# A list scheduler inside the kernel sets the order of every engine and the buffer of every tile

## The chip, the cores and the metric

The kernel runs on one core of a Trainium2 chip. The metric is the device time of one execution in microseconds (us). Before the change the median of three runs is 337.51 us (337.26 to 338.6).

The engines of the core are named as the profile names them: PE (TensorE, the matrix multiplier; PEld is its loading of weights), ACT (ScalarE), DVE (VectorE), POOL (GpSimd) and SP (SyncE, which issues the transfers of inputs and outputs). Each takes its instructions strictly in the order in which the program lists them; an instruction that has to wait holds up everything behind it on the same engine.

## The reference, cut to what matters

```
f = sigmoid(f_logit)                                   # q, k, v, f_logit: (4, 8, 768, 48)
for t in range(768):
    state = f[t][:, None] * state + outer(k[t], v[t])  # state: (4, 8, 48, 48)
    y[t]  = q[t] @ state
x = y as rows of 384 (8 heads x 48)                    # (3072, 384)
p = domain_probs / sum(domain_probs)                   # 4 experts
out = sum over e of p[:, e] * (relu(x @ w1[e]) @ w2[e])   # w1: 384 x 1024, w2: 1024 x 384
```

A gated linear attention is followed by four small two-layer networks (experts), all four of which are computed for every row and added up with weights p.

## The kernel before

Time is cut into C = 6 chunks c of T = 128 steps; each has B = 4 batches b. For one chunk and one batch the attention is a chain across the engines:

- `gate` (ACT, Exp and Ln; for two batches at once in all chunks but the first) makes log-gates `gp`.
- `pe_cs` (PE) sums them up over time; `exps` (ACT: `eQ`, `eK`, `egs`) makes the factors.
- `products` multiplies q and k by them (`qp`, `kp`; the q product on DVE in chunk 0 and on POOL later, the k product always on POOL); `cast_v` makes `vb`.
- `pe_tp` (PE) transposes both, `ev_tp` (DVE) copies them out of PSUM (`QK`).
- `pe_at` (PE) makes the 128 x 128 products of all heads (`A`), `ev_at` (DVE) masks them (`AT`), one instruction for eight heads.
- `pe_y` (PE) makes the output from `AT`, `vb` and the state of the chunk before, `ev_y` (ACT) copies it (`yb`); `pe_xt` transposes it and `ev_xt` (ACT) copies it into `xT`, the input of the experts.
- `pe_kv` (PE), `ev_kv` (DVE) and `state` (POOL, four instructions) carry the state into the next chunk.

The experts of a chunk are "units" of PE work: 8 h units per expert (`mm_h`, three matmuls of 128x512, result `hp`; the relu goes to DVE for three of eight and to ACT for the others) and 8 o units per expert (`mm_o`, four matmuls of 128x384, result `op`; every second one is followed by its scaling into `o_sb`, on ACT for the first expert and on DVE for the others). An h unit for half of the batches has 128x256 matmuls.

The order is written out by hand. `first_attention` places the steps of chunk 0 at times that are sorted. From then on `units(c)` lists the units of chunk c, alternating h of one expert with o of the expert before, and the attention of chunk c+1 hangs on the units as `steps`: after unit i come the steps that were put at i. Chunk 1 is different: its batches 0 and 1 (LO) go at the end of chunk 0 (steps 29 to 39), its batches 2 and 3 (HI) go into the first units of chunk 1 itself, whose experts 0 and 1 are done for LO first and for HI after (L355 to L359, L443 to L448), and chunk 2 follows from unit 18 of chunk 1 (L437).

Transfers: SP issues all inputs (`load`), first those of chunk 0 one batch at a time, then f, k, q, v of chunks 1 and 2, two batches at a time; later chunks are issued when chunk c starts. The f load of chunk 1 waits for the sixth weight transfer, and with it, being first, everything behind it on SP (L414, L415). The eight weight transfers (`weights`, w1 and w2 of four experts, cast to bf16 on the way) are issued by POOL, after the last k product of chunk 0; the first of them waits for the last k load of chunk 0.

PSUM has eight banks: two for `hp`, two for `op`, two for the small attention results (`pt`) and two for `A`.

## Time and profile before

| what | value |
|---|---|
| median of three runs | 337.51 us (337.26 to 338.6) |
| the profiled execution: its own time | 336.81 us |
| the profiled execution: span from first to last instruction | 335.1 us |
| granted TensorE clock, mean over the span | 0.995 |
| PE busy | 309.5 us (92%), 2304 matmuls |
| DVE / ACT / POOL busy | 159.5 / 148.7 / 95.8 us |
| bytes moved | 30.31 MB |

In the rows quoted below, a timeline row has the start in us from the beginning of the span, the duration in us, engine, source line, operation, output and inputs, the shape, the number of equal instructions merged (x), and in brackets how long the engine had been idle before and what ended that. Matmuls overlap in the records, so the time from the start of one row to the start of the next is the price of it. A row of the windows has the stretch, its length, and for each engine the busy time and the number of instructions in it; then the granted TensorE clock, the DMA share and GB/s. A row of the groups has the number of instructions and after the bar their busy time in us, the mean of one in ns, and the idle time before them.

### The profile page before, as it was taken

What the parts mean: (1) busy time and instruction counts of PE and PEld (TensorE: products, weight loads), DVE (VectorE), ACT (ScalarE), POOL (GpSimd) and SP (SyncE); (2) the same over time, 40 slices, a digit from 0 to 9 for tenths busy, and PEclk for the clock granted to TensorE, in tenths of its full rate; (3) what the DMA queues carried; (4) which work ended last, traced back from release to release, by engine and by line L of the source; (5) the groups of instructions that cost most, each with busy time, mean ns of one, the idle gap of its engine ahead of it and who ended that gap; (6) DMA issues with size and microseconds to landing.
All of it is one profiled execution on the core that took longest, in us unless ns stands there. A gap on an engine that the chain in (4) does not pass through costs nothing.

```text
span 335.1 us, 5754 instructions
## 1 busy us (share of the span) xinstructions
PE 309.5 (92%) x2304; PEld 181.2 (54%) x2304; DVE 159.5 (48%) x259; ACT 148.7 (44%) x299; POOL 95.8 (29%) x164
## 2 busy tenths in 40 slices
PE   2859999976859999999999999999999999999995
PEld 2634555544637665555655555655555555555552
DVE  5664233463533665444565354566454454422442
ACT  5633432607474533645433735533735434244220
POOL 5293400235445532243432143422142200000000
PEclk9999999999998999999999999999999999999999
DMA  8989999999892089022098020000020000110002
GB/s 163 213 116 207 208 202 207 221 206 253 157 210 49 2 163 167 23 72 49 3 186 144 23 72 0 2 2 1 23 73 0 3 0 2 47 49 0 0 2 94
DMA packets 111531, 30.31 MB, mean 90 GB/s; under 512 B 102800, under 2 KB 109968, under 8 KB 111504
## 3 DMA queue, kind: packets, MB, share of 16 engines
q1 hardware_dynamic: 105744, 23.65, 35.6%
q0 software_dynamic: 5760, 6.29, 11.2%
q8 instruction: 18, 0.29, 0.4%
q14 instruction: 9, 0.07, 0.1%
HBM read 31.51 MB, written 4.72 MB: 108 GB/s over the span
## 4 chain that ended last, share of the span: by engine, by line
PE 86%; ACT 4%; DMA 3%; DVE 3%; POOL 3%; issue 1%; POOLq 0%; DVEq 0%; ACTq 0%
PE hp L304 38%; PE op L320 36%; PE pt L194 3%; DMA w_sb<-in_moe_w_dram 2%; PE A L212 2%; POOL kp L177 2%; PE pt L247 1%; PE pt L233 1%; PE pt L229 1%; PE pt L150 1%; PE pt L273 1%; ACT eQ L161 1%; DVE Sf L257 1%; ACT ex L141 1%; DMA fg<-in_f_logit_dram 1%
## 5 line engine op out<-in xcount | busy, mean ns | idle before, releaser
L304 PE MATMUL hp<-xT,w_sb 128*128 128x512 bf16 (+1 forms) x624 | 159.5, 368 | 4.4 <-ACT xT L279 1.1
L320 PE MATMUL op<-w_sb,h_sb 128*128 128x384 bf16 x768 | 154.9, 326 | 0.0
L312 ACT ACTIVATE h_sb<-hp 128x512 bf16<-128x512 f32 (+1 forms) x130 | 73.5, 566 | 98.6 <-PE hp L304 92.5
L320 PEld LDWEIGHTS <-h_sb 128*128 128x128 bf16 x768 | 74.7, 98 | 65.9
L304 PEld LDWEIGHTS <-w_sb 128*128 128x128 bf16 x624 | 57.0, 100 | 45.3 <-issue 7.2
L310 DVE TENSOR_SCALAR h_sb<-hp 128x512 bf16<-128x512 f32 (+1 forms) x78 | 50.6, 649 | 54.8 <-PE hp L304 48.4
L330 DVE SCALAR_TENSOR_TENSOR o_sb<-op,pn,o_sb 128x384 f32<-128x384 f32 x72 | 44.4, 617 | 67.7 <-PE op L320 60.3
L175 POOL TENSOR_TENSOR qp<-qg,eQ 128x384 bf16<-128x384 f32 x20 | 19.9, 997 | 105.2 <-ACT eQ L161 76.8
L265 POOL TENSOR_TENSOR Sf<-Sf,egs 48x192 f32<-48x192 f32 x40 | 20.1, 503 | 52.2 <-DVE Sf L257 50.0
L218 DVE TENSOR_TENSOR AT<-A,mask 128x1024 bf16<-128x1024 f32 x24 | 29.3, 1222 | 8.2 <-PE A L212 7.9
L201 DVE COPY QK<-pt 112x1024 bf16<-112x1024 bf16 x24 | 16.6, 690 | 21.8 <-PE pt L194 21.8
L177 POOL TENSOR_TENSOR kp<-kg,eK 128x384 bf16<-128x384 f32 x24 | 24.1, 1004 | 9.8 <-ACT egs L168 9.8
L239 ACT CAST yb<-pt 128x384 bf16<-128x384 f32 x24 | 11.6, 483 | 25.2 <-PE pt L233 25.2
L257 DVE TENSOR_TENSOR Sf<-Sf,pt 48x192 f32<-48x192 f32 x40 | 14.1, 352 | 15.4 <-PE pt L247 14.6
L279 ACT COPY xT<-pt 128x384 bf16<-128x384 bf16 x20 | 9.5, 477 | 22.5 <-PE pt L273 22.5
L327 ACT ACTIVATE o_sb<-op,pn 128x384 f32<-128x384 f32 x24 | 14.0, 584 | 9.2 <-PE op L320 8.6
L161 ACT ACTIVATE eQ<-pt 128x384 f32<-128x384 f32 x20 | 9.8, 490 | 15.4 <-PE pt L153 11.6
L266 POOL CAST sb<-Sf 48x192 bf16<-48x192 f32 x40 | 13.6, 340 | 2.6
L233 PE MATMUL pt<-vb,AT 128*128 128x48 bf16 x192 | 12.0, 190 | 1.7 <-DVE vb L185 1.7
L194 PE MATMUL pt<-ident,qp 128*112 128x128 bf16 x96 | 10.8, 241 | 2.4 <-DVE qp L175 2.0
L194 PEld LDWEIGHTS <-qp 128*112 128x112 bf16 x96 | 9.4, 146 | 5.8 <-DVE qp L175 2.9
L194 PE MATMUL pt<-ident,kp 128*112 128x128 bf16 x96 | 10.8, 241 | 1.8 <-POOL kp L177 1.8
(52 smaller groups left out, 177.6 us busy)
## 6 DMA issues: line engine op xcount, KB each, us to landing
w_sb<-in_moe_w_dram POOLq DMA_DIRECT2D x8, 768.0 KB, 17.1
out_dram<-o_sb SPq DMA_DIRECT2D x24, 192.0 KB, 1.9
fg<-in_f_logit_dram SPq DMA_DIRECT2D x10, 384.0 KB, 5.8
kg<-in_k_dram SPq DMA_DIRECT2D x10, 384.0 KB, 5.8
qg<-in_q_dram SPq DMA_DIRECT2D x10, 384.0 KB, 5.8
vg<-in_v_dram SPq DMA_DIRECT2D x10, 384.0 KB, 5.6
fg<-in_f_logit_dram SPq DMA_DIRECT2D x4, 192.0 KB, 3.7
kg<-in_k_dram SPq DMA_DIRECT2D x4, 192.0 KB, 3.8
```

Source lines behind the costliest of these rows:

```text
L175: lead.tensor_tensor(out=Qpad[c % NB][:, b, :, 0:D], in0=t["q"][:, bs, :], in1=eQ.rearrange("t (h d) -> t h d", d=D), op=ALU.mult)
L177: nc.gpsimd.tensor_tensor(out=Kpad[c % NB][:, b, :, 0:D], in0=t["k"][:, bs, :], in1=eK.rearrange("t (h d) -> t h d", d=D), op=ALU.mult)
L194: nc.tensor.transpose(out=tp[:, j, i, :], in_=src[:, b, 2 * i:2 * i + 2, :].rearrange("t h d -> t (h d)")[:, 0:MP], identity=ident)
L201: nc.vector.tensor_copy(out=QK, in_=t["tp", b])
L218: nc.vector.tensor_tensor(out=AT.rearrange("s r i t -> s (r i t)"), in0=t["A", b].rearrange("s r i t -> s (r i t)"), in1=mask01, op=ALU.mult)
L257: nc.vector.tensor_tensor(out=Sf[ps, b], in0=Sf[ps, b], in1=KV[ps, :, r, :], op=ALU.add)
L265: nc.gpsimd.tensor_tensor(out=Sf[ps, b], in0=Sf[ps, b], in1=eg, op=ALU.mult)
L304: nc.tensor.matmul(out=hp[:, n0:n1], lhsT=w1_sb[:, e, kk, fc * 128:(fc + 1) * 128], rhs=t["xT"][:, kk, n0:n1], start=(kk == 0), stop=(kk = ...
L310: nc.vector.tensor_relu(out=hs[:, fc, n0:n1], in_=hp[:, n0:n1])
L312: nc.scalar.activation(out=hs[:, fc, n0:n1], in_=hp[:, n0:n1], func=AF.Relu)
L320: nc.tensor.matmul(out=op, lhsT=t["h", e][:, fc, nt * T:(nt + 1) * T], rhs=w2_sb[:, e, fc, :], start=(fc == 0), stop=(fc == KF - 1))
L330: nc.vector.scalar_tensor_tensor(out=o, in0=op, scalar=pe, in1=o, op0=ALU.mult, op1=ALU.add)
```

## The change

Each step of the kernel becomes an `Op` of a `Plan`: with the engines that may run it and its estimated duration on each, a priority, the steps it depends on, the buffers it takes and the buffers it frees. `Plan.run` steps through an estimated time: whenever an engine is free, it takes the step of lowest priority number whose dependencies have ended, plus a latency of 0.2 us to another engine and another 0.2 us behind PE steps, and for which buffers are free. What comes out is the order in which everything is issued, the engine for the steps that may run on several, and the buffer of each tile. "DMA" is one more engine of the plan, which moves one transfer at a time.

Beside the order, these things change:

- `A` is split by r into two banks and its mask into two DVE instructions of 128x512; the attention has a pool of four single banks (`ps_t`) for everything.
- The q and k products and the v cast of chunks 0 and 1 may run on POOL or DVE; the copies `yb` and `xT`, the relu and the scaling of the first expert may run on ACT or DVE. ACT is asked first, so most relus go to ACT.
- `qp`, `kp`, `vb` have 6, 7 and 7 one-batch buffers, `gp` and the inputs four two-batch buffers. Twenty memsets on DVE at the beginning instead of nine.
- The steps of `pe_kv` of chunk 0 stand in its attention, not between its first h units.
- Chunk 1 is planned as four batches in a row, as early as its inputs are estimated to be there, and not as two by two.
- Only the first f load of chunk 1 still depends on the sixth weight transfer.

The core of the diff:

```diff
--- before.py
+++ after.py
...
+    LATENCY = 0.2
...
+    def ready(self, o, e):
+        t = 0.0
+        for d in o.deps:
+            if d.end is None:
+                return None
+            t = max(t, d.end + d.lag + (self.LATENCY if d.engine != e else 0.05))
+        return t
...
+    def take(self, o):
+        new = [k for k in o.takes if k not in self.slot]
+        for r in {k[0] for k in new}:
+            if len(self.rooms[r]) < sum(k[0] == r for k in new):
+                return False
+        for k in new:
+            self.slot[k] = self.rooms[k[0]].pop(0)
+        return True
...
+        left = sorted(self.ops, key=lambda o: o.prio)
+        free_at = {e: 0.0 for o in left for e in o.costs}
+        freeing, done, now = [], [], 0.0
+        while left:
+            for f in [f for f in freeing if f[0] <= now + 1e-9]:
+                freeing.remove(f)
+                self.rooms[f[1]].append(f[2])
+            for e in free_at:
+                while free_at[e] <= now + 1e-9:
+                    for o in left:
+                        if e in o.costs:
+                            t = self.ready(o, e)
+                            if t is not None and t <= now + 1e-9 and self.take(o):
+                                break
+                    else:
+                        break
+                    left.remove(o)
+                    o.engine, o.start, o.end = e, now, now + o.costs[e]
+                    free_at[e] = o.end
+                    for k in o.frees:
+                        self.left[k] -= 1
+                        if self.left[k] == 0:
+                            freeing.append((o.end + self.LATENCY, k[0], self.slot[k]))
+                    done.append(o)
...
-    io = ctx.enter_context(tc.tile_pool(name="io", bufs=2))
...
+    rooms = {"ps_h": 2, "ps_o": 2, "ps_t": 4, "f": 4, "q": 4, "k": 4, "v": 4, "ex": 2, "gp": 4, "e": 2, "qp": 6, "kp": 7,
+             "vb": 7, "egs": 8, "QK": 2, "AT": 2, "yb": 2, "xT": 2, "h": 2, "o": 8}
+    P = Plan(rooms)
...
-    mask01 = const.tile([T, H * T], FP32)
+    mask01 = const.tile([T, NP * T], FP32)
...
+        ins[c, nm, b] = nc.sync.dma_start(out=tl(nm, c, b // 2)[:, hh(b, n), :],
+                                          in_=srcs[nm][c, :, b * H:(b + n) * H, :])
+        if (c, nm, b) == (1, "f", 0):
+            after(ins[c, nm, b], ins["w", 5])
...
+        nc.vector.tensor_tensor(out=tl("AT", c, b)[:, r].rearrange("s i t -> s (i t)"),
+                                in0=tl("A", c, b, r).rearrange("s i t -> s (i t)"), in1=mask01, op=ALU.mult)
...
+    def add_load(c, nm, b, n, prio, deps=()):
+        op = P.add(f"ld {nm}{c}.{b}", {"DMA": 1.05 * n}, lambda e: load(c, nm, b, n), prio,
+                   deps=deps, takes=[(nm, c, b // 2)], lag=2.0)
+        for i in range(n):
+            ld[c, nm, b + i] = op
+        return op
...
+    for i, (e, which) in enumerate(nw):
+        iss = P.add(f"w issue {i}", {"POOL": 0.9}, lambda _, i=i, e=e, which=which: load_w(i, e, which),
+                    -500 + i, deps=[ld[0, "k", B - 1]])
+        wd[e, which] = wd[i] = P.add(f"w {i}", {"DMA": 4.8}, lambda _: None, -500 + i, deps=[iss], lag=2.0)
+    for half in range(2):
+        for j, nm in enumerate("fkqv"):
+            add_load(1, nm, 2 * half, 2, -400 + 4 * half + j, deps=[wd[5]] if half == 0 and j == 0 else [])
...
+            cs = P.add(f"cs {c}.{b}", {"PE": 0.36 if more else 0.17}, on(pe_cs), s(0),
+                       deps=[G[b]], takes=[pt_("cs")], lag=0.2, frees=[("gp", c, half)])
+            ex = P.add(f"exps {c}.{b}", {"ACT": 1.1}, on(exps), s(0) + 0.1, deps=[cs],
+                       takes=[("e", c, b)] + ([("egs", c, b)] if more else []), frees=[pt_("cs")])
+            pe = {"POOL": 1.0, "DVE": 0.56} if c < 2 else {"POOL": 1.0}
+            qm = P.add(f"q {c}.{b}", pe, one(product, 0), s(4) - 0.2,
+                       deps=[ex, ld[c, "q", b]], takes=[("qp", c, b)], frees=[("q", c, half), ("e", c, b)])
+            km = P.add(f"k {c}.{b}", pe, one(product, 1), s(4) - 0.1,
+                       deps=[ex, ld[c, "k", b]], takes=[("kp", c, b)], frees=[("k", c, half), ("e", c, b)])
+            vb = P.add(f"v {c}.{b}", {"POOL": 0.5, "DVE": 0.36} if c < 2 else {"POOL": 0.5}, one(cast_v), s(4),
+                       deps=[ld[c, "v", b]], takes=[("vb", c, b)], frees=[("v", c, half)])
...
+            eA = [P.add(f"ev_at{r} {c}.{b}", {"DVE": 0.7}, on(ev_at, r), s(7) + 0.1 + 0.1 * r, deps=[at],
+                        takes=[("AT", c, b)], frees=[pt_("A", r)]) for r in range(2)]
+            y = P.add(f"y {c}.{b}", {"PE": 0.4 if c else 0.28}, on(pe_y), s(11), deps=eA + [vb, kvdone.get((c - 1, b))],
+                      takes=[pt_("y")], frees=[("QK", c, b), ("AT", c, b), ("vb", c, b)], lag=0.2)
+            ey = P.add(f"ev_y {c}.{b}", {"ACT": 0.48, "DVE": 0.56},
+                       lambda e, b=b: copy(e, tl("yb", c, b), tl("y", c, b)[:, 0:HD]), s(11) + 0.1,
+                       deps=[y], takes=[("yb", c, b)], frees=[pt_("y")])
...
+                kvdone[c, b] = P.add(f"state {c}.{b}", {"POOL": 1.75}, on(state), s(15) + 0.2,
+                                     deps=[ek, ex], frees=[("egs", c, b)])
...
+        m = P.add(f"h {c}.{e}.{fc}.{n0}", {"PE": 0.645 * n / NT}, lambda _: mm_h(c, e, fc, n0, n1), p,
+                  deps=[wd[e, 1]] + [xdone[c, b] for b in xs], takes=[key], lag=0.2, frees=[("xT", c)])
+        hdone[c, e, fc, n0] = P.add(f"relu {c}.{e}.{fc}.{n0}",
+                                    {"ACT": 0.6, "DVE": 0.69} if n == NT else {"ACT": 0.39, "DVE": 0.42},
+                                    lambda g: relu(c, e, fc, n0, n1, g), p - 3, deps=[m],
+                                    takes=[("h", c, e)], frees=[key])
...
-    def weights():
-        for w in ((0, 1), (1, 1), (0, 2), (2, 1), (1, 2), (3, 1), (2, 2), (3, 2)):
-            w_ins.append(load_w(*w))
-        after(w_ins[0], k_last)
...
+    attention(0, lambda b, s: -200 + 3.6 * b + s * 0.8, 1)
...
+            base = u0 + (0 if c else 10)
+            attention(c + 1, lambda b, s, base=base: base + 2 + 5 * b + s, 2)
...
+    done = P.run()
...
+    for o in done:
+        o.emit(o.engine)
...
```

What this does to the lists is shown at three places, before and after.

POOL, from its first product to the second weight issue (`w1_sb`, `w2_sb` are the weights, `Sf` and `egs` belong to `state`). Before:

```order
L177 TENSOR_TENSOR kp0_131<-kg_92,eK_161 128x8x48
L177 TENSOR_TENSOR kp0_131<-kg_92,eK_189 128x8x48
L177 TENSOR_TENSOR kp0_131<-kg_92,eK_240 128x8x48
L177 TENSOR_TENSOR kp0_131<-kg_92,eK_297 128x8x48
L124 DMA w1_sb_148<-in_moe_w1_dram 128x3x1024 x2
```

After:

```order
L257 TENSOR_TENSOR qp0_92<-q0_136,e0_151 128x8x48
L257 TENSOR_TENSOR qp1_94<-q0_136,e1_183 128x8x48
L261 CAST vb0_224<-v0_162 128x384
L257 TENSOR_TENSOR kp2_108<-k1_196,e0_208 128x8x48
L257 TENSOR_TENSOR qp2_96<-q1_215,e0_208 128x8x48
L308 TENSOR_TENSOR Sf_121<-Sf_121,egs0_154 48x192
L309 CAST sb1_125<-Sf_121 48x4x48
L308 TENSOR_TENSOR Sf_121<-Sf_121,egs0_154 48x192
L309 CAST sb1_125<-Sf_121 48x4x48
L225 DMA w1_sb_130<-in_moe_w1_dram 128x3x1024 x2
```

POOL's part of the fourth batch went to DVE, and the state of batch 0 stands ahead of the weights.

SP, behind the load of the probabilities (`pt` in both), where chunk 1 begins. Before:

```order
L83 DMA pt_110<-in_moe_domain_probs_dram 128x24x4
L70 DMA fg_390<-in_f_logit_dram 128x16x48
L70 DMA kg_392<-in_k_dram 128x16x48
L70 DMA qg_394<-in_q_dram 128x16x48
L70 DMA vg_396<-in_v_dram 128x16x48
```

After:

```order
L359 DMA pt_127<-in_moe_domain_probs_dram 128x24x4
L218 DMA k2_338<-in_k_dram 128x16x48
L218 DMA f2_675<-in_f_logit_dram 128x16x48
L218 DMA q2_696<-in_q_dram 128x16x48
L218 DMA v2_714<-in_v_dram 128x16x48
```

The k load now stands ahead of the f load, which is the one that waits for the weights.

ACT, from the second factors of chunk 1's LO batches on (`eQ_776` before, `e1_763` after) to the Ln of the next gate or two. Before:

```order
L161 ACTIVATE eQ_776<-pt_770 128x384
L163 ACTIVATE eK_778<-pt_770 128x384
L168 ACTIVATE egs_759<-pt_770 112x4
L239 CAST yb_875<-pt_857 128x384
L239 CAST yb_906<-pt_888 128x384
L279 COPY xT_924<-pt_920 128x3x128
L279 COPY xT_924<-pt_926 128x3x128
L312 ACTIVATE h_sb_947<-hp_943 128x256
L312 ACTIVATE h_sb_947<-hp_954 128x256
L141 ACTIVATE ex_959<-fg_390 128x768
L143 ACTIVATE gp1_133<-ex_959 128x16x48
```

After:

```order
L251 ACTIVATE e1_763<-ps_t3_743 128x384
L252 ACTIVATE e1_763<-ps_t3_743 128x384
L254 ACTIVATE egs5_766<-ps_t3_743 112x4
L236 ACTIVATE ex1_804<-f3_735 128x768
L240 ACTIVATE gp3_90<-ex1_804 128x16x48
L251 ACTIVATE e0_857<-ps_t2_839 128x384
L252 ACTIVATE e0_857<-ps_t2_839 128x384
L254 ACTIVATE egs6_860<-ps_t2_839 112x4
L251 ACTIVATE e1_878<-ps_t1_845 128x384
L252 ACTIVATE e1_878<-ps_t1_845 128x384
L254 ACTIVATE egs7_881<-ps_t1_845 112x4
L212 COPY xT1_927<-ps_t1_908 128x3x128
```

The gate of the HI batches (`ex`, `gp`) moved from behind the LO batches' `xT` and two relus to ahead of them, and `yb` went to DVE.

More of the change, by code (lines that the diff above doesn't have):

```diff
@@ L61 @@
-    cur = {}
-    def load(c, names, b0, b1):
-        t = cur.setdefault(c, {})
-        ins = []
-        for nm in names:
-            if nm not in t:
-                t[nm] = io.tile([T, B * H, D], FP32, name=nm + "g")
-            hs = slice(b0 * H, b1 * H)
-            ins.append(nc.sync.dma_start(out=t[nm][:, hs, :], in_=srcs[nm][c, :, hs, :]))
-        return ins
-    def after(later, earlier):
-        tc.add_manual_dep(later.ins, earlier.ins.name,
-                          mybir.DependencyInfo(mybir.DependencyClass.Sync, mybir.DependencyReason.DATA),
-                          reason="order of transfers")
@@ new lines, in after, with flat, hh, copy @@
+    def after(later, earlier):
+        tc.add_manual_dep(later.ins, earlier.ins.name,
+                          mybir.DependencyInfo(mybir.DependencyClass.Sync, mybir.DependencyReason.DATA),
+                          reason="order of transfers")
+    def flat(t, i):
+        return t[:, 2 * i:2 * i + 2, :].rearrange("t h d -> t (h d)")
+    def hh(b, n=1):
+        return slice((b % 2) * H, (b % 2 + n) * H)
+    def copy(eng, out, in_):
+        if eng == "ACT":
+            nc.scalar.copy(out=out, in_=in_)
+        else:
+            engines[eng].tensor_copy(out=out, in_=in_)
```

522 lines of the change are left out of this document (232 added, 290 removed).

## The prediction

> **What bounds the kernel now.** I read the page first, then the busy time by stages, then the timeline of the stages that are not full.
>
> ```profile
> span 335.1 us, 5754 instructions
> PE 309.5 (92%) x2304; PEld 181.2 (54%) x2304; DVE 159.5 (48%) x259; ACT 148.7 (44%) x299; POOL 95.8 (29%) x164
> PE   2859999976859999999999999999999999999995
> ```
>
> PE bounds it: 92% busy, the others below half. The slices show where it isn't full: the first three (to 25 us), slices 8 to 12 (59 to 101 us), and the last. By stages:
>
> ```profile
> 25.00:33.40 8.40, 8.25 (x39) 3.81 (x40) 3.89 (x9) 2.99 (x5) 2.80 (x8) 1.00 1.21 207
> 33.40:64.20 30.80, 30.80 (x172) 16.39 (x170) 11.43 (x19) 12.72 (x21) 3.96 (x10) 1.00 1.22 209
> 64.20:104.00 39.80, 29.87 (x302) 21.08 (x300) 17.58 (x31) 19.42 (x47) 18.66 (x31) 0.96 1.08 200
> 100.00:102.00 2.00, 1.48 (x10) 1.12 (x9) 0.42 (x1) 0.98 (x4) 1.99 (x3) 0.54 0.63 122
> 102.00:104.00 2.00, 2.00 (x19) 1.67 (x17) 1.12 (x2) 0.38 (x1) 0.41 (x1) 0.60 0.50 102
> 119.20:325.20 206.00, 206.00 (x1484) 116.56 (x1483) 99.92 (x154) 91.76 (x175) 46.83 (x80) 1.00 0.21 45
> ```
>
> From 119.2 to 325.2 PE has no idle time: nothing is to be had there, only lost. The hole is 64.2 to 104, the passage from chunk 0 to chunk 1: 39.80 - 29.87 = **9.93 us idle**, and 4 us at a granted clock of 0.54 and 0.60. No engine is full there. What PE waits for:
>
> ```profile
> 69.70 0.43 PE L194 MATMUL pt<-ident,kp 128*112 128x128 bf16 x4 [0.52 <-POOL kp L177]
> 72.62 0.40 PE L212 MATMUL A<-QK 48*128 48x128 bf16 x8 [0.75 <-DVE AT L218]
> 79.48 0.83 ACT L141 ACTIVATE ex<-fg 128x768 f32<-128x768 f32 x1
> 81.24 0.32 PE L150 MATMUL pt<-gp,Ub 128*128 128x384 bf16 x1 [1.63 <-ACT gp L143]
> 95.91 0.84 ACT L141 ACTIVATE ex<-fg 128x768 f32<-128x768 f32 x1
> 97.67 0.32 PE L150 MATMUL pt<-gp,Ub 128*128 128x384 bf16 x1 [1.12 <-ACT gp L143]
> 99.55 0.49 PE L304 MATMUL hp<-xT,w_sb 128*128 128x256 bf16 x3 [1.05 <-ACT h_sb L312]
> 56.36 1.58 SPq L70 DMA_DIRECT2D fg<-in_f_logit_dram  x1
> 63.38 1.82 SPq L70 DMA_DIRECT2D fg<-in_f_logit_dram  x1
> fg<-in_f_logit_dram SPq DMA_DIRECT2D x10, 384.0 KB, 5.8
> ```
>
> Links of the attention chain follow each other with too little PE work between. Yet the HI gate starts at 79.48 although its f load was issued at 56.36 and, by the median of 5.8, landed at 62; chunk 2's (issued 63.38, landed about 69) starts at 95.91. The hand-written order, not a transfer, holds them.
>
> **The start.** This changes most in order, and costs.
>
> ```profile
> 14.75 0.68 SPq L83 DMA_DIRECT2D pt<-in_moe_domain_probs_dram  x1
> 18.23 1.71 POOL L124 DMA_DIRECT2D w_sb<-in_moe_w_dram  x2
> 24.39 0.48 ACT L279 COPY xT<-op 128x384 bf16<-128x384 bf16 x1 [0.59 <-PE op L273]
> 25.10 4.43 PE L304 MATMUL hp<-xT,w_sb 128*128 128x512 bf16 x12 [0.75 <-DMA w_sb<-in_moe_w_dram]
> 29.56 1.46 PE L304 MATMUL hp<-xT,w_sb 128*128 128x512 bf16 x6
> 31.27 1.46 PE L304 MATMUL hp<-xT,w_sb 128*128 128x512 bf16 x6
> 6.42 1.00 POOL L177 TENSOR_TENSOR kp<-kg,eK 128x384 bf16<-128x384 f32 x1 [2.09 <-ACT egs L168]
> L201 DVE COPY QK<-pt 112x1024 bf16<-112x1024 bf16 x24 | 16.6, 690 | 21.8 <-PE pt L194 21.8
> L310 DVE TENSOR_SCALAR h_sb<-hp 128x512 bf16<-128x512 f32 x66 | 45.5, 690 | 39.2 <-PE hp L304 34.1 <-ACT ex L141 4.2
> L175 DVE TENSOR_TENSOR qp<-qg,eQ 128x384 bf16<-128x384 f32 x4 | 2.2, 558 | 3.2 <-ACT eQ L161 2.6 <-DMA qg<-in_q_dram 0.6
> L257 DVE TENSOR_TENSOR Sf<-Sf,pt 48x192 f32<-48x192 f32 x40 | 14.1, 352 | 15.4 <-PE pt L247 14.6
> L185 DVE CAST vb<-vg 128x384 bf16<-128x384 f32 x4 | 1.5, 376 | 0.0
> L218 DVE TENSOR_TENSOR AT<-A,mask 128x1024 bf16<-128x1024 f32 x24 | 29.3, 1222 | 8.2 <-PE A L212 7.9
> L265 POOL TENSOR_TENSOR Sf<-Sf,egs 48x192 f32<-48x192 f32 x40 | 20.1, 503 | 52.2 <-DVE Sf L257 50.0 <-ACT o_sb L327 0.3
> L312 ACT ACTIVATE h_sb<-hp 128x512 bf16<-128x512 f32 x110 | 65.8, 598 | 89.0 <-PE hp L304 82.9 <-DVE o_sb L330 5.2 <-ACT xT L279 0.4
> L330 DVE SCALAR_TENSOR_TENSOR o_sb<-op,pn,o_sb 128x384 f32<-128x384 f32 x72 | 44.4, 617 | 67.7 <-PE op L320 60.3
> ```
>
> The first h unit needs both the first weights (issued 18.23, waited for until 25.10) and the last `xT` (24.39 + 0.48). Half a mask instruction appears in no row: at least 1.22 / 2 = 0.61, and for the same shape read from PSUM the relu's 0.69. I take 0.69, so a pair costs 0.16 more, 3.8 us over 24, all beside other work except in the two stages computed here.
>
> DVE's new list from its first product to the fourth mask holds four products (2.23), four QK copies (2.76), eight half masks (5.52), three casts (1.13), six state additions (2.11): 13.75 us. Ready at 6.4 (the factors, as POOL's first product at 6.42 shows), it ends at 20.2 if DVE never waits. Followed hop by hop, with each producer's row, it ends at 23.5: the q transposes of batches 0 to 2 now stand behind the next batch's `pe_cs`, and masks 2 and 3 stand behind state additions. From the mask four steps are left (y, copy, transpose, copy), about half a microsecond each as the last is (0.48 at 24.39), with hops 2.2: first h at **25.7**, between 22.4 and 27. POOL's `state` of batch 0, in front of the weights, waits for the first state addition (13.9 by the same walk) and is four instructions of at most 0.50; the weights are issued at 15.9 instead of 18.23. The old 6.87 to the wait's end makes 22.8; the k load of chunk 1, now issued right behind `pt` at 15.4, may cost them up to the 1.8 us in which SP issues one such load (rows at 56.36 and 63.38: four in 7.02), 24.6. So `xT` ends last: +0.6.
>
> Here the Trainium skill speaks against the change. "DMA: Bandwidth & Descriptors", section "Issuing engines are not separate DMA queues", has transfers of all issuing engines on the same 16 DMA engines, interleaved. By it the first weights pay the k load in full, 24.6 rather than 22.8; the sum would stay, since `xT` is later either way.
>
> Until the first o unit the old order did 8 h units, from 25.10 to 33.4, the first 12 matmuls at 0.37 each and then pairs of units in 1.7 (29.56 to 31.27). With all relus on ACT the two `hp` banks allow the same rate, and the list has 11 h units ahead of the first o: three at 0.82 instead of the 0.65 that an alternating unit takes, +0.5. The four `pe_kv` (0.2 each, a third of the y with kv below) no longer stand among the h units; half of them hid in the waits for banks there, so -0.4. **Start: +0.7**, from -2.5 to +2.5.
>
> **The hole.** Starting at the first `pe_cs` of chunk 1, PE's list up to the first h unit of chunk 1 has 6 cs, 1 h, 9 o, 4 pairs of transposes, 3 A, 2 y with kv, 2 xt.
>
> ```profile
> 64.19 0.33 PE L150 MATMUL pt<-gp,Ub 128*128 128x384 bf16 x1
> 64.54 0.81 PE L320 MATMUL op<-w_sb,h_sb 128*128 128x384 bf16 x4
> 65.19 0.33 PE L150 MATMUL pt<-gp,Ub 128*128 128x384 bf16 x1
> 116.85 0.21 PE L229 MATMUL pt<-sb,QK 112*128 112x96 bf16 x1
> 117.46 0.81 PE L304 MATMUL hp<-xT,w_sb 128*128 128x512 bf16 x3
> ```
>
> From start to start: cs 0.35, o 0.65, y with kv 0.61; transposes 8 x 0.055 = 0.45, A 0.33, xt 0.2, estimated at these rates. Sum 13.0 us. DVE's list there up to the second `yb` (three more products, one cast, three scalings, three QK, two masks, one state addition, two `yb`, at most 0.62 by the same shape above) is 11.2 us; it starts 1.6 after the first cs, waits about 0.3 for factors, then needs 1.4 more (QK and a state addition) to free the banks, and 0.7 follows to the first h: 15.1. PE idle **2.0** there. In the next 6.4 us DVE has 6.7 us of list, PE idle 0.7; the rest of chunk 1's halves 0.5. The inputs are there: HI's v was issued three loads behind the row at 56.36, 61.6, now one load earlier, and lands about 66; it is needed at 73. I take 4.0 for 3.2, because every hop was counted at its median: 9.93 - 4.0 = **-5.9** (from -1 to -7).
>
> The slow clock at 100 to 104 followed 6 us in which PE was half idle. PE's 3.48 busy us at a mean of 0.57 are 2.0 at 1: **-1.4** (0 to -1.5), if no such stretch remains; the walk's longest gap is 0.8. "TensorE: Matmul & The Clock Gate", Part 1, in the Trainium skill has the clock halved after a window of about 3.4 us without activity; the trace's longest gap here is 1.63, yet its clock fell. By the page alone no dip would follow either.
>
> **The full stage.** From chunk 3 on PE's list is nearly the old one. ACT takes about 50 more relus (0.6 each) among its gates and factors; a few h units of chunk 1 follow each other directly. **+0.7** (0 to +3). The tail is unchanged.
>
> **Sum.** 336.81 (the profiled execution; span 335.1 and 1.7 around it) + 0.7 - 5.9 - 1.4 + 0.7 = 330.9. The timed median is 0.7 above that execution; I say **331.2**.
>
> **Rivals.** (1) DVE bounds the hole: its list, 11.2 of 15 us and then full, slips by 0.2 per hop over some 20 hops; 4 us come back, 335.0. For it: masks and state additions gate every bank. Against: DVE was busy only 17.58 of 39.80. Chance 0.15. (2) The inputs bound it after all, and the plan only moves idle time: DMA share 1.08 in the hole, w6 and chunk 1 behind each other. Against: no PE wait there names a transfer. 336.8 + 0.7 = 337.5; 0.12. (3) Slower: ACT becomes the late engine of the full stage. A bank is wanted again after four alternating units of 0.65, so a relu may end 1.3 us late (2.6 less one unit and 0.6) before PE stops; a gate's two steps take 1.7 (79.48 to 81.24). With 14 batches' factors and 6 gates left, 0.5 each would be 10 us: 341; it is slower than before from 0.4 each on. Against: the list puts a relu between most of these steps. 0.11. (4) The forecast: 0.62.
>
> A measurement of this kernel tells about 0.5%, 1.7 us, from no change. Faster: forecast and (1), 0.77; same 0.12; slower 0.11. The forecast's own range is 328 to 334.5 from the bounds above; with (1) and part of (2) it reaches to 336.5.
>
> **What would show it.** Right: first h between 25 and 26.5, weights issued near 16; idle time of PE from first cs of chunk 1 over the next 40 us at 3 to 5; no granted clock below 0.9 there; the HI gate before the LO `xT`. Wrong: first h behind 28, or PE waits on DVE `QK`, `AT`, `Sf` above 6 us in sum, or idle PE behind 119 us in rows that name ACT `h`.

## The result: 4.2% faster, more than twice the forecast

| | median of the runs, us | profiled execution, us | its span, us |
|---|---|---|---|
| before | 338.0 (337.26 to 338.6) | 336.81 | 335.1 |
| changed | 323.81 (323.4 to 324.66) | 324.19 | 322.5 |

The ratio is 0.9584, with a 95% interval of 0.9552 to 0.9617; a second series of five rounds gave 323.68 and 0.9567 (0.9548 to 0.9585). Forecast were 331.2 and a range of 327.3 to 336.5: the sign was right, but the gain came out at 14.2 us and not 6.8 (338.0 less 331.2), and outside the range. In the table of experiments below two executions are left out as slow, one of e1 (638.17 us) and one of e4 (337.8 us). Against the profiled execution, from which the sum was made, the changed kernel is 12.6 us shorter.

The page of the changed kernel:

```profile
span 322.5 us, 5781 instructions
PE 306.1 (95%) x2304; PEld 181.3 (56%) x2304; DVE 142.1 (44%) x271; ACT 169.1 (52%) x326; POOL 92.6 (29%) x160
PE   1979999998999999999999999999999999999995
```

The slices of the hole, at 7, 6, 8 and 5 before, are at 9, with one 8. The same stages as before (columns: length, then busy time and count of PE, PEld, DVE, ACT and POOL, granted clock, DMA share, GB/s):

```profile
64.20:104.00 39.80, 37.86 (x477) 29.24 (x476) 35.87 (x69) 25.69 (x65) 29.82 (x52) 1.00 1.07 209
104.00:119.20 15.20, 15.20 (x122) 9.53 (x121) 6.90 (x12) 9.96 (x21) 7.95 (x12) 1.00 1.19 198
119.20:312.00 192.80, 192.80 (x1334) 107.78 (x1333) 72.38 (x126) 97.89 (x176) 33.40 (x55) 1.00 0.12 31
```

PE idles for 1.94 us of the hole instead of 9.93, does 477 instructions there instead of 302, and the granted clock stays at 1.00. All waits of PE between 60 and 105 us are these:

```profile
68.00 0.43 PE L265 MATMUL ps_t<-ident,qp 128*112 128x128 bf16 x4 [0.66 <-DVE qp L257]
76.58 0.23 PE L273 MATMUL ps_t<-QK 48*128 48x128 bf16 x1 [0.18 <-DVE Sf L301]
77.17 0.38 PE L273 MATMUL ps_t<-QK 48*128 48x128 bf16 x7 [0.36 <-DVE yb L214]
77.77 0.33 PE L313 MATMUL ps_t<-ident,yb 128*128 128x128 bf16 x3 [0.22 <-DVE QK L214]
78.62 0.32 PE L244 MATMUL ps_t<-gp,Ub 128*128 128x384 bf16 x1 [0.53 <-ACT xT L212]
```

The start, from the timelines of POOL, PE's weight loads, ACT and PE:

```profile
16.32 6.77 POOL L225 DMA_DIRECT2D w_sb<-in_moe_w_dram  x8
24.90 0.10 PEld L317 LDWEIGHTS <-w_sb 128*128 128x128 bf16 x1 [0.34 <-DMA w_sb<-in_moe_w_dram]
24.86 0.48 ACT L212 COPY xT<-ps_t 128x384 bf16<-128x384 bf16 x1 [0.59 <-PE ps_t L313]
25.39 9.24 PE L317 MATMUL ps_h<-xT,w_sb 128*128 128x512 bf16 x28 [0.57 <-ACT xT L212]
```

**Where the 12.6 us are.** Idle time by the rows shrank by (335.1 - 309.5) - (322.5 - 306.1) = 9.2 us, the span by 12.6. So I compared the kernels at equal work: every unit of PE counts its cost from start to start (the prediction's figures: h 0.645, o 0.65, `pe_cs` 0.35 and so on), and I note when each kernel has done so much of it. The figures of the small units leave some choice; other values that the rows allow shift the differences by up to 0.5 us.

| PE work done | before | changed | difference |
|---|---|---|---|
| 40 us | 60.70 | 61.30 | +0.60 |
| 80 us | 116.63 | 104.28 | -12.35 |
| 288 us | 323.36 | 310.95 | -12.41 |
| end of span | 335.1 | 322.5 | -12.6 |

Everything is won between 40 and 80 us of work: 55.93 us before, 42.98 now, **-12.95**. In the 39.8 us of the hole the kernel before did 24.8 us of work and the changed one does 36.8: it lost 15.0 and loses 3.0. Of the 15.0 the rows show 9.93 as idle. The slow clock is another 1.48 (1.48 busy us at 0.54, 2.00 at 0.60). About 3.5 are shown neither way. Two pieces of the timeline of before tell where most of them go:

```profile
66.39 0.43 PE L194 MATMUL pt<-ident,qp 128*112 128x128 bf16 x4
67.34 0.43 PE L194 MATMUL pt<-ident,kp 128*112 128x128 bf16 x4 [0.53 <-POOL kp L177]
...
85.87 0.39 PE L194 MATMUL pt<-ident,qp 128*112 128x128 bf16 x4
86.09 0.39 PE L194 MATMUL pt<-ident,kp 128*112 128x128 bf16 x4
```

Back to back, four transposes take 0.22 (85.87 to 86.09), though their row is 0.39 long: its end lies behind the moment at which PE can go on. So after the row at 66.39 PE could have gone on at 66.61 and went on at 67.34. It lost 0.73; the bracket says 0.53. The hole of before has 13 waits, so 0.2 for each makes 2.6 of the 3.5; for the rest no row is shown.

### The profile page after: what moved, and what is told of

It reads as the page before. It is cut to its first block, busy times and chain, and to the rows that moved or that the text cites. A ratio compares the mean times of both kernels' runs of the same rounds, so it can differ in the third digit from the quotient of the medians.

```text
span 322.5 us, 5781 instructions
## 1 busy us (share of the span) xinstructions
PE 306.1 (95%) x2304; PEld 181.3 (56%) x2304; DVE 142.1 (44%) x271; ACT 169.1 (52%) x326; POOL 92.6 (29%) x160
## 4 chain that ended last, share of the span: by engine, by line
PE 89%; DVE 6%; issue 1%; ACT 1%; DMA 1%; DVEq 0%; ACTq 0%
PE ps_h L317 40%; PE ps_o L329 37%; PE ps_t L265 3%; PE ps_t L273 2%; DVE AT L277 2%; PE ps_t L288 1%; PE ps_t L244 1%; PE ps_t L313 1%; DVE kp L257 1%; PE ps_t L284 1%; PE ps_t L294 1%; PE ps_t L247 1%; DMA f<-in_f_logit_dram 1%; DVE QK L214 1%; DVE o L336 1%
## 5 line engine op out<-in xcount | busy, mean ns | idle before, releaser
L325 ACT ACTIVATE h<-ps_h 128x512 bf16<-128x512 f32 (+1 forms) x182 | 104.2, 573 | 114.1 <-PE ps_h L317 108.2
L317 PE MATMUL ps_h<-xT,w_sb 128*128 128x512 bf16 (+1 forms) x624 | 158.2, 367 | 0.7 <-ACT xT L212 0.6
L329 PE MATMUL ps_o<-w_sb,h 128*128 128x384 bf16 x768 | 154.1, 326 | 0.0
L329 PEld LDWEIGHTS <-h 128*128 128x128 bf16 x768 | 71.5, 98 | 53.1
L336 DVE SCALAR_TENSOR_TENSOR o<-ps_o,pn,o 128x384 f32<-128x384 f32 x72 | 44.4, 616 | 103.5 <-PE ps_o L329 102.3
L277 DVE TENSOR_TENSOR AT<-ps_t,mask 128x512 bf16<-128x512 f32 x48 | 31.1, 684 | 19.9 <-PE ps_t L273 19.7
L261 POOL CAST vb<-v 128x384 bf16<-128x384 f32 x20 | 10.5, 539 | 90.5 <-PE ps_t L294 47.9
L257 POOL TENSOR_TENSOR qp<-q,e 128x384 bf16<-128x384 f32 x21 | 21.2, 1014 | 40.8 <-ACT e L251 37.1
L214 DVE COPY QK<-ps_t 112x1024 bf16<-112x1024 bf16 x24 | 16.5, 686 | 16.5 <-PE ps_t L265 16.5
L257 POOL TENSOR_TENSOR kp<-k,e 128x384 bf16<-128x384 f32 x19 | 19.2, 1014 | 5.2 <-ACT egs L254 4.1
L251 ACT ACTIVATE e<-ps_t 128x384 f32<-128x384 f32 x24 | 11.8, 491 | 7.4 <-DVE AT L277 3.4
L288 PEld LDWEIGHTS <-AT 128*128 128x128 bf16 x192 | 10.5, 101 | 3.7 <-DVE AT L277 2.1
L252 ACT ACTIVATE e<-ps_t 128x384 f32<-128x384 f32 x24 | 11.8, 494 | 0.0
```

The source lines that it names most:

```text
L214: engines[eng].tensor_copy(out=out, in_=in_)
L257: engines[eng].tensor_tensor(out=tl(("qp", "kp")[j], c, b)[:, 0, :, 0:D], in0=tl("qk"[j], c, b // 2)[:, hh(b), :], in1=tl("e", c, b)[:, j] ...
L277: nc.vector.tensor_tensor(out=tl("AT", c, b)[:, r].rearrange("s i t -> s (i t)"), in0=tl("A", c, b, r).rearrange("s i t -> s (i t)"), in1= ...
L288: nc.tensor.matmul(out=y[:, h * D:(h + 1) * D], lhsT=AT[:, r, i, :], rhs=vb[:, h, :], start=(c == 0), stop=True, skip_group_check=True)
L317: nc.tensor.matmul(out=tl("ps_h", c, e, fc, n0)[:, n0:n1], lhsT=w1_sb[:, e, kk, fc * 128:(fc + 1) * 128], rhs=tl("xT", c)[:, kk, n0:n1], s ...
L325: nc.scalar.activation(out=dst, in_=src, func=AF.Relu)
```

## Experiments

Four theories were tried: COVER (HI's chain runs early), BANKS (four single banks and half masks), ENGINES (products, copies and relus go to any free engine), and UNITS (how the idle time is to be counted). To keep the start apart, the table has the span less the start of the first h unit, both from the profiled execution (e7's for e1 and e7; the ratio there is e1's). Each ratio is taken to executions of the kernel before in the same series, whose medians lie between 337.9 and 338.2.

| run | us (median) | ratio to before [95%] | first h | span less first h |
|---|---|---|---|---|
| before | 338.0 | | 25.10 | 310.0 |
| changed | 323.81 | 0.958 [0.955, 0.962] | 25.39 | 297.1 |
| e2 HI late | 327.43 | 0.965 [0.962, 0.969] | 25.05 | 300.6 |
| e3 A whole | 325.81 | 0.962 [0.960, 0.965] | 28.77 | 295.2 |
| e4 engines fixed | 332.02 | 0.983 [0.978, 0.988] | 35.35 | 295.0 |
| e5 engines fixed from chunk 1 | 324.07 | 0.958 [0.956, 0.961] | 25.35 | 297.2 |
| e6 = e2 + e3 + e5 | 332.67 | 0.984 [0.981, 0.987] | 28.66 | 302.6 |
| e10 = e2 + e5 | 327.92 | 0.970 [0.966, 0.974] | 25.42 | 301.4 |
| e11 = e3 + e5 | 328.57 | 0.973 [0.970, 0.977] | 28.67 | 297.6 |
| e12 chunk 2 late | 324.5 | 0.960 [0.958, 0.963] | 25.09 | 298.1 |
| e13 HI and chunk 2 late | 325.51 | 0.963 [0.960, 0.966] | 25.34 | 298.8 |
| e1, e7 by hand: HI early | 338.24, 338.32 | 0.999 [0.996, 1.002] | 25.55 | 311.1 |
| e14 by hand: HI, chunk 2 early | 334.2 | 0.990 [0.986, 0.993] | 25.05 | 307.1 |
| e15 by hand: gates only | 333.15 | 0.986 [0.983, 0.988] | 25.19 | 305.7 |

### How idle time must be counted (e8)

```
-    rooms = {"ps_h": 2, "ps_o": 2, ...
+    rooms = {"ps_h": 1, "ps_o": 2, ...
```

> The changed kernel with one PSUM bank for the h units instead of two, planned anew: nearly each of the 224 h units now has to wait for the relu of the one before, so that the kernel has some 200 short waits where it had a dozen. PE's work is the same. This measures how the idle time of PE has to be counted. Theory UNITS (a wait costs its bracket and about 0.2 us more, because the row of the last matmul before it ends behind the moment at which PE could have issued the next): with a span that grows by G (40 to 100 us), the idle time of PE by the rows (span less PE's busy time) grows by 25 to 50 us less than G, 0.1 to 0.25 for each wait. Theory ROWS (the brackets are the whole loss): the idle time by the rows grows by G, within 5 us.

Its page:

```profile
span 389.3 us, 5778 instructions
PE 324.4 (83%) x2304; PEld 182.6 (47%) x2304; DVE 134.8 (35%) x259; ACT 174.7 (45%) x337; POOL 93.3 (24%) x161
```

The longest line of PE's waits (us in total, times, longest):

```profile
PE ps_h L317 <- ACT h L325: 43.6, 70, 0.7
```

Two h units from PE's timeline, the first at the slower pace, the second at the full one:

```profile
35.62 1.44 PE L317 MATMUL ps_h<-xT,w_sb 128*128 128x512 bf16 x3 [0.69 <-ACT h L325]
...
39.08 0.81 PE L317 MATMUL ps_h<-xT,w_sb 128*128 128x512 bf16 x3
```

The span grew by 66.8, the idle time by the rows by (389.3 - 324.4) - 16.4 = 48.5. The same 2304 matmuls were "busy" for 18.3 us more. There were 92 waits and not 200 (the plan mostly put o units between), 77 more than the changed kernel has, so the 18.3 fell short of the 25 expected. About 2 of it is a slower pace up to 38.7 us (last section); the rest is 0.2 a wait. UNITS holds, ROWS falls. The Trainium skill, "Perfetto Trace Analysis", section "Tensor Engine Instruction", has the end of a TensorE row estimated and not observed, which agrees.

### One part of the change put back (e2 to e5)

e2 adds a dependence to HI's gate (`lo` is a step of no length behind the third h unit of chunk 1). e3 has A whole in one tile (`ps_a`) and masks it in one instruction. e4 gives each step its old engine; the lines for q of chunk 0 (DVE), v, `yb`, `xT` and the first o are changed alike:

```
 e2  g1 = P.add(f"gate1 {c}.{b0}", ...
-              deps=[ld[c, "f", b0]], ...
+              deps=[ld[c, "f", b0]] + ([lo[0]] if (c, b0) == (1, 2) else []), ...
 e3
-    rooms = {"ps_h": 2, "ps_o": 2, "ps_t": 4, ...
+    rooms = {"ps_h": 2, "ps_o": 2, "ps_t": 2, "ps_a": 1, ...
 e4
-    {"ACT": 0.6, "DVE": 0.69} if n == NT else ...
+    ({"DVE": 0.69} if n == NT else ...) if fc in (1, 4, 6) else ({"ACT": 0.6} if n == NT else ...)
-    {"POOL": 1.0, "DVE": 0.56} if c < 2 else {"POOL": 1.0}
+    {"POOL": 1.0}
```

> The changed kernel, with one dependence more: the gate of HI (batches 2 and 3 of chunk 1) waits in the plan for the third h unit of chunk 1, about where it stands in the kernel before; everything else is planned anew around it. COVER: 4 to 9 us slower than the changed kernel (328 to 333). BANKS or ENGINES: at most 2 us slower (324 to 326), because the new banks and the free choice of engines are all still there. UNITS: as in the run before.

> The changed kernel with the banks of the kernel before: A as one tile of two banks of its own, masked in one instruction of 1.22 us, and two single banks for all other steps of attention; the plan is made anew for that. BANKS: 4 to 9 us slower than the changed kernel (328 to 333), most of it between 64 and 104 us. COVER or ENGINES: at most 2 us slower (324 to 326). In the stage that is full (behind 119 us) all theories expect no change: PE stays at its issue rate.

> The changed kernel with the engine of each step fixed as before: products and casts of chunk 1 on POOL, of chunk 0 with k on POOL and q and v on DVE; copies of y and xT on ACT; relus of units 1, 4 and 6 of 8 on DVE, the others on ACT; the first o of a row on ACT. Order and banks are planned anew around that. ENGINES: 4 us or more slower than the changed kernel (328 and above). COVER or BANKS: at most 2 us slower (324 to 326); DVE, at 35.9 busy of 39.8 us in the hole, would be relieved by it.

None brings the hole back. e2 costs 3.6, between its two ranges. e3 loses 3.4 at the start and nothing behind it: BANKS is worth a start, not a hole. e4 is 8.2 slower, which is within the range of ENGINES, but the loss is not in the hole: its first h unit comes 10.0 later, and nothing is lost behind it. Its timelines of POOL, PE and DVE:

```profile
15.47 6.78 POOL L225 DMA_DIRECT2D w_sb<-in_moe_w_dram  x8 [2.23 <-DMA k<-in_k_dram]
24.26 0.99 POOL L257 TENSOR_TENSOR kp<-k,e 128x384 bf16<-128x384 f32 x1
25.31 0.67 PE L265 MATMUL ps_t<-ident,kp 128*112 128x128 bf16 x4 [4.86 <-POOL kp L257]
28.57 0.25 DVE L230 TENSOR_REDUCE psm<-pt 128x24 f32<-128x96 f32 x1 [8.86 <-DMA pt<-in_moe_domain_probs_dram]
31.21 0.61 PE L273 MATMUL ps_t<-QK 48*128 48x128 bf16 x8 [5.23 <-DVE QK L214]
```

The last k product stood on POOL behind eight weight issues, and then the `QK` copy on DVE behind the sum of the probabilities, whose transfer landed 13.7 us after it was issued and not after the plan's 0.3 + 2.0 us. A plan is as good as its estimates, and an engine that works in order passes a wrong one on. So the engines were fixed from chunk 1 on alone:

> The changed kernel with the engine of each step fixed as before from chunk 1 on; chunk 0 keeps the free choice, so that the start is the changed kernel's again. With every engine fixed, the run before lost 9 us, but its trace has them before 40 us: a product of the last batch stood on POOL behind the eight weight issues. START (all of that loss was there): within 1.5 us of the changed kernel, 322.5 to 325.5, with the first h at 25 to 26. ENGINES (the free choice in chunk 1 matters too): 326 or above.

START is confirmed: 324.07, the same as the changed kernel. The hole of e5:

```profile
64.20:104.00 39.80, 38.09 (x482) 29.65 (x481) 28.11 (x56) 28.45 (x71) 33.61 (x56) 1.00 1.12 210
```

DVE is relieved from 35.87 to 28.11 us and nothing changes. DVE does not bound the hole, however full it looks.

### All put back but the order (e6, e10, e11)

> The scheduler with everything else put back: A whole in two banks of its own, engines fixed as before from chunk 1 on, the gate of HI behind the third h unit of chunk 1. What is left of the change is that the plan sets the order. Theory ORDER (any banks and engines will do once a plan fills the links): the whole A costs 3.4 us at the start (first h near 28.8) and HI's lateness 3.6, so 326 to 331. Theory RESOURCES (banks, engines and HI's place can each stand in for the others, which is why none of the three alone brought the hole back): without all three the hole is back, 333 to 339.

> HI's gate late and the engines fixed from chunk 1 on, with the new banks and half masks. Of the two runs with one of these alone, the first was 3.6 us slower than the changed kernel and the second 0.3; with the old banks added, 8.9 slower, of which 3.3 at the start. ADDITIVE with the rest coming from the old banks: 327 to 329. ENGINES MATTER ONCE HI IS LATE (with HI's chain alone in the hole there is nothing to hide a slow product or copy behind): 330 or above.

> The old banks (A whole in two banks of its own) and the engines fixed from chunk 1 on, with HI planned early. The whole A costs 3.4 us at the start. If the planned order closes the hole as long as HI is early: 325.5 to 327.5, first h near 28.7 and the idle time of PE between 64 and 104 us below 2.5. If banks and engines together are needed: 329 or above, with waits of PE in the hole that name DVE or ACT copies.

e11 (between its two ranges) has old banks and old engines, so that the planned order, HI early included, is what remains. Behind the first h unit it takes 297.6 against 310.0 before and 297.1 with the whole change: order alone gives 12.4 of 12.9, or 10.5 if the 1.9 by which e3's late start flatters this measure is taken off. Counted at equal work, where a late start flatters nothing, e11 takes only 0.3 us more than the changed kernel from 40 to 80 us of work, so the higher figure is the better one. (The buffers of the changed kernel, one batch at a time, stay in e11; no run puts them back.) Its start costs 3.3. e6, which came out at 332.67 between its two theories, has HI late as well and still keeps 7.4. e10 says the loss is additive with HI late, and part of it is the clock; e10's windows:

```profile
74.00:76.00 2.00, 0.94 (x16) 0.73 (x17) 1.38 (x3) 1.89 (x4) 1.47 (x4) 1.00 1.44 196
76.00:78.00 2.00, 1.47 (x17) 1.18 (x16) 0.70 (x2) 1.87 (x6) 1.08 (x3) 0.59 1.39 218
78.00:80.00 2.00, 1.96 (x10) 1.33 (x10) 0.41 (x1) 1.21 (x4) 1.86 (x4) 0.50 1.35 202
80.00:82.00 2.00, 2.00 (x15) 1.74 (x14) 0.36 (x2) 1.84 (x4) 2.00 (x3) 0.50 1.49 188
82.00:84.00 2.00, 2.00 (x23) 1.30 (x21) 1.30 (x3) 1.34 (x3) 1.50 (x3) 0.70 1.40 203
```

Busy time times what is missing to 1.00 gives 3.2 us here; by the same working it is 1.7 in e2 and 3.0 in e6, and none in the changed kernel. In these three runs a good part of what "HI late" costs is thus the slow clock that follows its waits.

### Is it the early chains, or the filling? (e12, e13, e14)

e12 and e13 hold the gates of chunk 2 as `lo` holds HI's above. e1 is the kernel before with HI's gate at unit 33 of chunk 0 and HI's steps from its unit 36 on (those beyond its end at the first units of chunk 1), where they stood at 2 and at 3 to 15 of chunk 1; e7 is the same kernel, run again. e14 adds chunk 2:

```
 e1
-    for s, at in ((0, 3), (4, 9), (7, 11), (11, 13), (13, 15)):
+    for i, s in enumerate((0, 4, 7, 11, 13)):
+        at = 36 + 2 * i + b - 2
 e14, besides
-    base = 2 if c > 1 else 18
+    base = 2 if c > 1 else 8
```

> The kernel before with its hand-written order, and one thing moved: the gate and the five steps of batches 2 and 3 (HI) of chunk 1 start at unit 36 of chunk 0, behind those of LO, instead of at unit 3 of chunk 1. Banks, masks and the engine of every step stay as before. Theory COVER (the hole closed because HI's chain now runs while PE still has units of chunk 0 and of LO): 5 to 9 us faster than before, 329 to 333. Rival BANKS (it closed because four single banks and half masks free PE sooner) and rival ENGINES (it closed because products, copies and relus go to whichever engine is free): at most 2 us faster, 336 to 338, because the moved steps then queue for the same two banks and the same engines. Theory UNITS (how idle time must be counted: a row of PE ends about 0.2 us behind its last issue, so each wait costs more than its bracket shows): the change of the time is the change of the span minus work at issue rate, and at least a third more than the change of PE's idle time by the rows.

> The hand-written order with HI's chain early once more, for a trace in which PE runs at its full rate. Time as measured before (338, no gain). If COVER is right and something took the gain back, the idle time of PE moves: less between 76 and 84 us, more elsewhere, in rows whose releaser is named. If HI's chain never got through early, the HI h units are as late as before.

> The changed kernel with the gates of chunk 2 held behind the first two h units of HI in chunk 1, where they stand in the kernel before (95.91 and 97.52 there; 74.46 and 83.38 in the changed kernel); HI early, banks and engines free. Theory CHUNK2 (chunk 2's chain is the work that fills the hole): 3 us or more slower than the changed kernel, 327 and above. Theory FILL (the plan puts something into every link, whatever is at hand): at most 2 us slower, 323.5 to 326.

> The changed kernel with both chains held where they stand in the kernel before: HI's gate behind the third h unit of chunk 1, chunk 2's gates behind the first two h units of HI. HI late alone was 3.6 us slower than the changed kernel. CHUNK2 (both chains early are the gain): most of the gain is gone, 333 to 338. FILL: 326 to 330.

> The kernel before, by hand: HI's chain from unit 36 of chunk 0 on (alone it gave nothing, 338) and chunk 2's attention from unit 8 of chunk 1 on instead of unit 18. CHUNK2: faster than before by 4 us or more (334 and below), since chains placed early are what the gain consists of. FILL: a place in a list with fixed distances leaves the waits within each chain, so at most 3 us faster (335 to 339).

Under the plan it matters little where the chains stand: of the 14.2 us, 0.7 are lost with chunk 2 late and 1.7 with both late. The 1.7 are less than FILL allowed, and less than the 3.6 of HI late alone, where the trace has chunk 2's gate at 74.15 ahead of HI's at 78.50. By hand, HI early gives nothing, and both early give 3.9, between the ranges. COVER and CHUNK2 fall as the whole cause; most of it is FILL. e7 shows where HI's gain went. By the rows PE waits 9.2 us between 60 and 106 us, in the kernel before 9.4: HI's gate costs no wait any more, but the links of HI's chain behind it do (the first two rows), and the waits at the next gates, those of chunk 2, are as long as before (the last two):

```profile
80.94 0.43 PE L194 MATMUL pt<-ident,qp 128*112 128x128 bf16 x4 [0.91 <-POOL qp L175]
84.23 0.40 PE L212 MATMUL A<-QK 48*128 48x128 bf16 x8 [0.69 <-DVE AT L218]
98.49 0.32 PE L150 MATMUL pt<-gp,Ub 128*128 128x384 bf16 x1 [1.12 <-ACT gp L143]
100.37 0.49 PE L304 MATMUL hp<-xT,w_sb 128*128 128x256 bf16 x3 [1.05 <-ACT h_sb L312]
```

And e13 shows the filling: ACT's gate of HI, almost as late as in the kernel before (79.48), then PE up to its reader:

```profile
77.53 0.83 ACT L236 ACTIVATE ex<-f 128x768 f32<-128x768 f32 x1
78.40 0.84 ACT L240 ACTIVATE gp<-ex 128x768 bf16<-128x768 f32 x1
...
78.42 0.81 PE L329 MATMUL ps_o<-w_sb,h 128*128 128x384 bf16 x4
79.08 0.49 PE L317 MATMUL ps_h<-xT,w_sb 128*128 128x256 bf16 x3
79.40 0.81 PE L329 MATMUL ps_o<-w_sb,h 128*128 128x384 bf16 x4
80.05 0.33 PE L244 MATMUL ps_t<-gp,Ub 128*128 128x384 bf16 x1
```

PE works until the factors are there and then takes `pe_cs` without a wait. In the hand-written order one h unit of half width (0.33 us) stood there, and PE waited 1.63.

### What the gates cost by hand (e15)

The first line stands in the list of chunk 0; the lines behind the dots belong to chunk 1:

```
+                steps.setdefault(34, []).append(([lambda: gate(1, 2, 4)], []))
...
-                steps.setdefault(2, []).append(([lambda: gate(1, 2, 4)], []))
-                    steps.setdefault(base - 2 + half, []).insert(
+                    steps.setdefault(base - (7 if c == 1 else 2) + half, []).insert(
```

> The kernel before with two ACT steps moved and PE's order untouched: HI's gate from behind the third h unit of chunk 1 to unit 34 of chunk 0, chunk 2's gates five units earlier. Theory DISTANCE (a gate of 1.7 us stood 0.33 us ahead of its reader): PE's waits of 1.63 and 1.12 on the gates go, and with them the 1.05 and 0.52 on relus that stood behind the gates on ACT, about 4.3 by the rows, 0.2 more for each (UNITS), and the slow clock at 100 to 104 (1.4) if it came from these gaps: 331.5 to 334.5. Rival CHAIN (behind the gate the next link is late as well, and PE waits there instead): 335.5 to 338.

The time is 333.15 us: DISTANCE holds. Three gates, six instructions, moved ahead of others on ACT, with PE's list untouched, give 4.8 of the 14.2 us. The rest stays in the other links. Of the three waits of e15 below, the first two are there in the kernel before too; the third is new, and a moved gate makes it: chunk 2's second gate keeps ACT until 90.91, and `yb` is copied behind it.

```profile
72.62 0.40 PE L212 MATMUL A<-QK 48*128 48x128 bf16 x8 [0.75 <-DVE AT L218]
88.73 0.40 PE L212 MATMUL A<-QK 48*128 48x128 bf16 x8 [0.88 <-DVE AT L218]
91.61 0.20 PE L229 MATMUL pt<-sb,QK 112*128 112x96 bf16 x1 [1.11 <-ACT yb L239]
```

### The start, and a last try (e9, e16, e17)

e9 emits the load `ld k1.0` behind `ld f1.0`; e16 does that and spaces the batches of an attention by 3 units of priority instead of 5.

> The changed kernel with one transfer moved: the k load of chunk 1, issued at 16.23 ahead of the weights, is issued behind chunk 1's f load (near 47) instead. No other engine's order changes. Theory SHARED (the transfers of SP and POOL share the same engines, so the k load delayed the first weights by the 1.7 by which their wait, 16.32 to 24.90, is longer than the 6.87 of before): PE's weight load stops waiting at 23.0 to 23.5, yet the first h unit stays at 25.2 to 25.5, since the last xT is copied at 24.86 + 0.48. Rival OWN (the queue of POOL runs apart and the weights were slow for another reason): the wait still ends near 24.9. Whole time by either: 323 to 325, if the k load is in time for its product near 66.

> The changed kernel with the k load of chunk 1 behind its f load, and the priorities of the batches of an attention 3 units apart instead of 5. The k load alone gave 323.03 in one look (first h 0.33 earlier); the closer batches are worth up to 0.9 by the plan's own estimate. Theory: 321.5 to 323.5, 0.5 to 2 us faster than the changed kernel beside it. Rival (both are noise): equal within 0.5 us.

> The changed kernel itself, unaltered, beside the run before: 323.4 to 324.7 as measured.

In e9 the weights were issued at 15.99, and PE's weight load waited for them until 24.48:

```profile
24.48 0.10 PEld L317 LDWEIGHTS <-w_sb 128*128 128x128 bf16 x1 [0.25 <-DMA w_sb<-in_moe_w_dram]
```

The k load among the changed kernel's transfers of 14 to 30 us (KB each, us from issue to landing):

```profile
k<-in_k_dram SPq DMA_DIRECT2D x1, 384.0 KB, 23.1
```

8.49 us without the k load ahead, 8.58 with it: SHARED, with its price of 1.7, falls. The k load shares the engines, but it is the one that waits, 23.1 us (5.6 is the median of k's loads of this size). Why the first weights take 1.6 us longer than the 6.87 of before was not tested. The traces suggest the inputs of chunk 0: in e9 they still move 187 GB/s in the microsecond from 16 us, and the first weight packets come at 18; in the kernel before, the weights are issued at 18.23, when that traffic is down to 32 GB/s. The one execution of e9 took 323.03 us. e16 gave 323.22 (323.1 to 323.55), e17 beside it 323.68 (323.28 to 323.95), with ratios of 0.9557 [0.954, 0.9575] and 0.9567 [0.9548, 0.9585]: the intervals overlap, so no better version is shown.

## Why the forecast had the sign and missed the size

- **What bounds it: right.** PE bounds both kernels, no engine or transfer the hole. The hand-written order held the chain; e15 prices one part of that at 4.8 us.
- **Start +0.7: right, in part by luck.** +0.60 at 40 us of work, first h at 25.39 for 25.7, weights issued at 16.32 for 15.9. But the first h unit came only 0.29 later than before, and a term was missing: PE's slow pace at the start (last section) lasted until 30.4 us instead of 28.5, which costs about 0.8. That the weights end with the k load at 24.6 came near the row (24.90) for a reason that e9 refutes. The rule drawn on there (the Trainium skill, "DMA: Bandwidth & Descriptors", "Issuing engines are not separate DMA queues") holds as far as the transfers share engines; that the weights pay the k load in full does not follow. The half mask took 0.684, from 0.69.
- **Hole -5.9: this step failed.** It set an idle time by the rows (9.93) against a rest from a walk of start-to-start costs (4.0). The walk itself was good: from the first `pe_cs` of chunk 1 to its first h unit it had 15.1 us, and the trace has 15.9 (63.45 to 79.31). The figure that it was set against was too small. (By the rows PE idled 1.9 us, not the 3 to 5 named as the sign of being right.) In the walk's units the hole of before had lost 15.0, 13.5 without the clock. That is 3.5 us more to win; the rest of the walk was 3.0 and not 4.0, and between 104 and 119.2 another 0.9 came, which the sum left out. Measured in its place: -12.95 + 1.5 for the clock = **-11.4**. The mechanism held; what was mis-sized is what there was to win.
- **Clock -1.4: right** (-1.5). In e2, e6, e7 and e10 the slow clock comes back with the waits; e13, e14 and e15 have waits and kept 1.00 in the hole.
- **Full stage +0.7: nothing.** From 80 to 288 us of work both kernels take the same time within 0.3 us.
- With the hole at -11.4 the prediction's own sum is 336.81 + 0.7 - 11.4 - 1.4 + 0.7 = 325.4, 1.2 above the profiled 324.2. The range failed for the same reason: its lower end let the hole give at most 7.
- **Rivals.** DVE as the bound falls with e5: full in the hole (35.87 of 39.80), it can be relieved by 8 us for nothing. The inputs fall with the waits: none names a transfer there. ACT late in the full stage falls with 192.80 busy of 192.80.

## What to carry over

Measure what a stall costs from start to start against the same rows back to back, not from the brackets between PE's rows: each wait here cost about 0.2 us more than its bracket, and a stage that looked 25% idle had lost 38%. A distance in an order written by hand is a time, not a count: where units become half as long, what was far enough no longer is, and moving six instructions on an engine that is not the bound gave a third of what the scheduler gave. This scheduler's gain lay mostly in filling every link, wherever the chains stood, and its loss in the durations that it did not know (a transfer, eight weight issues on POOL).

## What the runs showed of the hardware

- **The slow clock needs no long pause, and comes in portions.** The traces' clock records have 0.50 for 3.41 us in before (from 100.18), e2 and e7, and for 6.83 us in e6 and e10; the stretches at 1.00 between are multiples of 3.41 as well (before: 71.68). The Trainium skill, "TensorE: Matmul & The Clock Gate", Part 1, has a window of about 3.4 us, which agrees with the lengths. It also has the clock fall after a window that was idle; no trace here shows one. In e10 the clock fell at 76.37, after 3.41 us in which PE was 2.12 busy, with no gap above 0.51. The busy time of PE alone does not decide it: e8 kept 1.00 behind 3.41 us with 1.61 busy (52.38 to 55.79). What does stays open.
- **A slow pace that the clock's column does not show.** In e8 an h unit takes 1.44 up to 37 us and 0.81 from 39 on, while the column reads 1.00 in every window. It reads so for want of a record: the clock records of e8 begin at 38.72 us, those of before at 28.50, those of the changed kernel at 30.37, and at these times the matmuls of an h unit go from 0.43 to 0.22 from start to start. With a wait behind each unit PE stayed at the slow pace for 13.7 us from its first h unit on; before, with its h units back to back, for 3.4, the changed kernel for 5.0.
- **A product on DVE takes longer beside one on POOL.** DVE's first product took 1.08 instead of 0.56 while POOL's ran; POOL's took 1.00, as it does alone. The Trainium skill, "GPSIMD Engine Reference", "Specifications", has the two contend when DVE reads two inputs from SBUF, which agrees. From the timeline of the changed kernel:

```profile
6.60 1.08 DVE L257 TENSOR_TENSOR kp<-k,e 128x384 bf16<-128x384 f32 x1 [1.73 <-ACT e L252]
...
6.27 1.00 POOL L257 TENSOR_TENSOR qp<-q,e 128x384 bf16<-128x384 f32 x1 [2.83 <-ACT e L251]
```
